# Joining the words of float64 weights on VectorE instead of GpSimd, in a transformer kernel on one core

## The chip, the core and the metric

The kernel runs on one core of a Trainium2 chip. A core has five engines, each with its own instruction queue, worked through in order: TensorE (PE in the profile, its weight loads PEld), VectorE (DVE), ScalarE (ACT), GpSimd (POOL) and SyncE (SP, which here issues transfers). Engines wait for each other by semaphores. The metric is the device time of one execution in microseconds (us).

## The reference

Eight batches of 576 tokens go through three layers, all in float32 (names as in the reference, shapes in brackets):

```
q_s = softmax(q) over d;  k_s = softmax(k) over the tokens      # 8 batches, 8 heads, 576 tokens, d = 64
x = (q_s @ (k_s^T @ v)), heads side by side                     # 576 x 512 for a batch
xn = (x - mean) / sqrt(var + 1e-6) * g_ln
x = x + relu(xn @ w_ch1) @ w_ch2                                # w_ch1 512 x 2048, w_ch2 2048 x 512
out = sum over 4 experts of gate * (causal attention of x) @ wo # the two best experts of each token count
```

`w_ch1` and `w_ch2` arrive as float64, which no engine computes in. The kernel reads them as pairs of 32-bit words and makes float32 numbers of them by integer operations.

## The kernel before, in words

Every float32 product is made of three fast products: an operand is split into a rounded upper part (ScalarE, a copy) and the rest, its lower part (a subtraction). The hidden layer's 2048 columns are 16 blocks `f` of 128. Phase 1 takes attention, normalisation and blocks 0 to 11 of the hidden layer for all batches; phase 2 takes the other blocks and the experts. For the last batch of phase 1 all 16 blocks are used.

**A block of weights** is 128 x 512 numbers (`Wide.pieces`); each `f` has two, one of `w_ch1` and one of `w_ch2`. Its steps: `size` (ScalarE, L245) takes the high word without its sign; `least` and `shift` (VectorE, L249, L253) bound it and rebase the exponent; `sign` (VectorE, L259) puts the sign back; `rest` (ScalarE, L256) rounds the low word to what is left of the mantissa; `whole` (L263, GpSimd) adds the two words as integers, here called **the join**; `big` (ScalarE, L266) makes the upper part; `small` (L270) makes the lower part, on VectorE for the blocks in `CDVE` and on GpSimd for the others. The first `Wide` has 24 blocks (numbers 0 to 23), converted at the start of the program; the second has 8 (numbered from 0 again), converted while the last batch of phase 1 is worked on.

**The start** (function `start`) covers the attention of batch 0 (pairs of heads 0 to 3), its normalisation, the 24 blocks, batch 0's products and, between them, the attention and normalisation of batch 1 (pairs 4 to 7). A planner in the program builds one list of operations with a cost for each, an engine and what each comes behind, and emits them by urgency; the order that it finds is then fixed for each engine (`in_order`), so an engine never passes a late instruction. The planner's costs are numbers in the code; changing one moves instructions.

The products of batch 0 come in 24 steps of about 3.2 us of TensorE: blocks 0 to 6 for the first half of the tokens (h = 0), the same for the second (h = 1), then blocks 7 to 11 for either half. In a step, `psh` is the first product, ScalarE and VectorE (L711, L714) make its two parts `hh`, and `acc` is the second product; L732 adds the sums to `x`. Step 18 (h = 0, block 11) is the last that needs newly converted weights.

**A normalisation** is the chain mean (`pmu`, TensorE) - subtract (L633, VectorE) - square (L639, ScalarE) - add up (L611, GpSimd) - split (`lnsum`, L615 and L618) - variance (`pvar`, TensorE) - root (L643 to L645, ScalarE) - refine (L650, L651, VectorE) - scale (L655, VectorE) - split into `xhl` (L660 ScalarE, L664 VectorE). The products of a half batch need its `xhl`.

**A pair of heads** needs the exponentials of q less their maximum, and their sums. For the pairs in `QACT` ScalarE does both in ten small instructions with an accumulator (L459); for the others GpSimd subtracts the maximum (L425), ScalarE takes one exponential (L437) and VectorE sums (L467).

Of the kernel before, what the change touches and what calls it, by code (L numbers as in the profile page):

```python
# [19 lines left out]
# Columns of the hidden layer (in blocks of 128) that the first phase works on; the second does the rest.  # L20
FSPLIT = 12
# Those of them that a batch's halves take in turn while the first batch is worked on
CHUNKS = (0, 7)
# Buffers of the blocks of weights that are being converted, and blocks loaded ahead of the one at work
TB, MIDB, AHEAD = 4, 4, 2
# Pairs of heads whose results come from float32 products, whose k loses its maximum on GpSimd, and whose exponentials
# of q come with their sums: at the start the other engines have more to do than the tensor engine.
WHOLE, KPOOL, QACT = 8, (0, 1, 5, 6, 7), (0, 1, 6, 7)
# Blocks of weights whose lower parts VectorE makes; GpSimd makes the rest.
CDVE = (1, 4, 7, 8, 9, 14, 16, 17, 18, 20, 21)  # L30
# Halves of batches (batch, half) whose means come from float32 products
DIRECT = ((0, 0),)
# The banks that come in turn for the first pairs of heads: the ring's, or one of the sums' before their first use
SPARE = (None, "acc0", "acc1", "acc2", None)
# The planner's times, in ns: of a step of the products, from one engine to another, behind loads; how much later than
# the first a more urgent piece may start, and one of these
# [4 lines left out]
# In which half-steps of the products the stages of a pair of heads and of a normalisation come, and from one of them  # L41
# to the next
UNIT_AT, UNIT_GAP = (0, 1, 2, 4, 5, 7), 4
NORM_AT, NORM_GAP = (0, 2, 4, 6, 8, 10), 8
# float32's least normal number: the first word of its float64 form, read as a float32
# [3 lines left out]
def weave(main, side):  # L49
    """Emits the pieces of `main`, with those of `side` spread evenly between them."""  # L50
    done = 0
    for i, piece in enumerate(main):
        piece()
        upto = (i + 1) * len(side) // len(main)
        for s in side[done:upto]:
            s()
        done = upto
    for s in side[done:]:
        s()


class Op:
    """A piece of work for one engine: about what it costs there and how long its result takes to the next engine, in ns,
    and what it comes behind."""
# [5 lines left out]
    def take(self, ring, *till):  # L70
        """Takes one of a ring's buffers, until `till` are done."""
        self.takes.append((ring, till))
        return self


def rush(ops):
    """Nothing but what these wait for is more urgent."""
    for op in ops:
        if op.end is None:
            op.late = min(op.late, RUSH)  # L80
            rush(op.deps)


def plan(ops, rings, which):
    """Has the pieces emitted in the order in which engines that do first what is most urgent would come to them."""
# [9 lines left out]
    while todo:  # L95
# [16 lines left out]
        # the most urgent piece of all that could start now, and then the most urgent one of its engine  # L112
# [17 lines left out]
def tile_kernel(ctx: ExitStack, tc: tile.TileContext, q, k, v, g_ln, w1, w2, w_gate, wq, wk, wv, wo, out):  # L130
# [15 lines left out]
    # Rows of a head in four interleaved chunks, and the last 128 of them in a fifth  # L146
# [17 lines left out]
    def in_order(instructions):  # L164
        """Each engine issues its instructions in this order."""
# [48 lines left out]
    class Wide:  # L214
        """Loads blocks of float64 numbers, as pairs of words with the low one first, rounds them to
        float32 and splits that."""
# [16 lines left out]
        def pieces(self):  # L233
            """The next block, piece by piece: the sign, the rebased exponent and the first 20 bits of the mantissa; the
            rest of it, rounded. Numbers under float32's normal range count as its least."""
# [26 lines left out]
            def whole():  # L262
                nc.gpsimd.tensor_tensor(box[0], box[0], low, op=ALU.add)  # L263
# [4 lines left out]
            def small():  # L268
                eng = nc.vector if n in CDVE else nc.gpsimd
                eng.tensor_tensor(lo, box[0].bitcast(F32), raw(h), op=ALU.subtract)  # L270
                while len(self.tiles) < min(n + 1 + self.ahead, len(self.blocks)):
                    self.load()
# [37 lines left out]
    # ------------------------------------------------------------------ phase 1  # L310
# [10 lines left out]
    def psy(name):  # L321
        if spare:
            # the sums' banks, before their first use
# [5 lines left out]
    # The first batch's last pairs of heads have buffers of their own, where weights lie later.  # L329
# [6 lines left out]
    def whole(n):  # L336
        """Whether a pair's result comes from float32 products: while the other engines have more to do than the tensor
        engine"""
# [18 lines left out]
    def next_unit(n):  # L357
        """The pair of heads that takes over a pair's buffers"""
# [36 lines left out]
    class Heads:  # L395
        """The linear attention of a pair of heads, in stages."""
# [16 lines left out]
        # Pieces of one engine's work each  # L413

        def k_rows(self):
            """The maximum of k's columns over each partition's rows"""
# [39 lines left out]
        def q_exps(self, j):  # L456
            """The exponentials, less the maximum, and their sums"""
# [23 lines left out]
        def q_parts(self, s):  # L481
            """The turned q, its rows back in order, as parts"""
# [34 lines left out]
        def kv_product(self):  # L517
            """k^T v, and the sums of k's columns"""
# [40 lines left out]
    def a_unit(n):  # L559
        """The work of a pair of heads, in stages, each behind the tensor engine's part of the last."""  # L560
# [31 lines left out]
    class Norm:  # L592
        """The normalisation of half a batch, in pieces of one engine's work each."""
# [8 lines left out]
        def add_x(self, c):  # L602
            """The sum of x's chunks"""
# [43 lines left out]
        def refine(self):  # L647
            """One Newton step to float32: r = r0 * (1.5 - 0.5 * ve * r0^2), here times -2"""
# [50 lines left out]
    class Step:  # L699
        """The products of half a batch with a block of the hidden layer, in pieces"""  # L700
# [27 lines left out]
        def add(self, c):  # L728
            """The residual and the sums so far"""
# [19 lines left out]
    def run_steps(steps, slots, wide):  # L749
        """The products of a list of (batch, half, block), the second of each behind the first of the next;  # L750
        slots: what else is emitted in each half of a step."""
# [23 lines left out]
    def front_slots(b):  # L775
        """When the stages of a batch's attention and normalisation are emitted, in halves of steps."""
# [49 lines left out]
    def start():  # L826
        """The first batch, the weights, and the second batch's attention and normalisation, as what is most urgent for
        the products comes first"""
# [16 lines left out]
        def unit(n):  # L845
# [22 lines left out]
            km = A("km", DVE, 740, head, [ldk, ldq])  # L868
# [45 lines left out]
            # no bank is held for want of a buffer  # L914
# [7 lines left out]
            # buffers  # L922
# [21 lines left out]
        def norm(b, h):  # L944
# [48 lines left out]
            # its reader comes later  # L993
            his[0].take("xhl", *([at["lastf", h]] if b == 0 else ()))

        # the weights
        nblocks = 2 * FSPLIT
        for k in range(nblocks):
# [11 lines left out]
            c0 = A(0, ACT, 520, g(0), [at.get(("w", k - 1, 0)), ld])  # L1010
            c1 = A(10, DVE, 340, g(1), [c0])
            c1 = A(1, DVE, 340, g(2), [c1])
            c2 = A(2, ACT, 520, g(3), [c0])
            c3 = A(3, DVE, 600, g(4), [c1])
            c5 = c4 = A(4, POOL, 1220, g(5), [c2, c3])
            c6 = A(6, ACT, 520, g(6), [c4])
            c7 = A(7, *((DVE, 600) if k in CDVE else (POOL, 1220)), g(7), [c6, at.get(("w", k - 1, 7))])
            c0.take("t", c7)
            ld.take("raw", c5)
        # the first batch's products  # L1020
# [33 lines left out]
        # the weights' second half lies where the first batch's buffers were  # L1054
# [7 lines left out]
        # From there on the sums' banks are theirs.  # L1062
# [73 lines left out]
    # ------------------------------------------------------------------ phase 2  # L1136
# [7 lines left out]
    # Adding 1e9 to the negated scores of later keys takes them out of the minimum.  # L1144
# [5 lines left out]
    # The last queries of two experts share the partitions; their mask, and their q between zeros.  # L1150
# [8 lines left out]
    # before[e, e'] = 1 where e' < e, after[e, e'] = 1 where e' > e  # L1159
# [21 lines left out]
    def mlp2(b, h, x2s):  # L1181
        """The rest of the feed-forward layers for half a batch, in pieces."""
# [36 lines left out]
    def psm(name):  # L1219
        """A bank; every so many come from those of the values' sums."""  # L1220
# [37 lines left out]
    def join(x2s, res):  # L1258
        """The block of tokens that lies in both halves"""
# [6 lines left out]
    def v_proj(x2s, res):  # L1266
        def one(c):
# [17 lines left out]
            # the last rows twice, for both parts of their weights  # L1285
# [8 lines left out]
        def gates(c0, c1):  # L1294
            """The top two of the experts' logits, and the softmax over them, for some blocks of tokens."""
# [34 lines left out]
    def layout(grp):  # L1330
        """Where the transposed weights of each block of keys lie, for the queries of a group."""
# [10 lines left out]
    class Unit:  # L1342
        """The attention of 128 queries over the earlier keys, for two experts."""
# [272 lines left out]
```

## Time and profile before

| | us |
|---|---|
| three runs: median | 1362.39 |
| lowest | 1358.6 |
| highest (disturbed) | 6870.57 |
| the profiled execution: its span (no other time of it is recorded) | 1355.0 |
| TensorE busy in the span | 1301.7 (96%) |
| VectorE, ScalarE, GpSimd busy | 888.9, 686.6, 343.5 |

The page's slices show where TensorE is not busy: the first four of 40 slices (about 135 us) have it at 5, 6, 7 and 8 tenths, and from there on it stands at 9 or more until the last slice. In the first four slices VectorE is at 7, 9, 9 and 9 tenths. So the time of the program is the time of the start, plus a stretch of some 1220 us in which TensorE is the limit and other engines do their work beside it. The lines shown further down are of three kinds: sums over a stretch, groups of equal instructions with their mean duration, and single instructions in order of time.

### The profile page before, as it was taken

How to read it: one execution, taken by the hardware profiler on the slowest of the kernel's cores; microseconds unless marked ns; L12 is line 12 of the kernel's file. 1: busy time of each engine (PE TensorE's matmuls, PEld its weight loads, DVE VectorE, ACT ScalarE, POOL GpSimd, SP SyncE). 2: the span in 40 equal slices, each digit the busy share in tenths (PEclk: the TensorE clock that was granted, in tenths of full speed). 3: DMA queues.
4: the chain of work that ended last, by engine and by line, in shares of the span. 5: the costliest groups of instructions: out<-in, count | busy, mean ns of one | idle time of the engine just before them, and what ended most of it. 6: DMA issues, size and time to landing. Idle time of an engine off the chain costs nothing.

```text
span 1355.0 us, 26225 instructions
## 1 busy us (share of the span) xinstructions
PE 1301.7 (96%) x9612; PEld 1268.8 (94%) x9612; DVE 888.9 (66%) x2602; ACT 686.6 (51%) x1802; POOL 343.5 (25%) x445
## 2 busy tenths in 40 slices
PE   5678999999999999999999999999999999999997
PEld 4577999999999999999999999999999999999996
DVE  7999564754645555545574238777768677776786
ACT  7667343443334433434442136656566656565666
POOL 5756323122121221212322002111211111121212
PEclk9889999999999999999999999999999999999999
DMA  8655232331321413315212023323232331423021
GB/s 230 198 173 150 80 111 56 117 94 45 110 75 67 109 58 123 84 50 158 65 34 48 1 77 126 107 82 106 82 97 87 86 105 59 115 86 90 23 67 55
DMA packets 136767, 124.78 MB, mean 92 GB/s; under 512 B 84160, under 2 KB 124096, under 8 KB 133056
## 3 DMA queue, kind: packets, MB, share of 16 engines
q1 hardware_dynamic: 126176, 97.16, 25.3%
q10 hardware_dynamic: 10464, 25.95, 5.2%
q8 instruction: 76, 1.25, 0.4%
q14 instruction: 51, 0.42, 0.1%
HBM read 74.07 MB, written 35.39 MB: 81 GB/s over the span
## 4 chain that ended last, share of the span: by engine, by line
PE 80%; DVE 12%; DMA 3%; ACT 2%; issue 1%; SPq 1%; POOL 1%; ACTq 0%; DVEq 0%; POOLq 0%
PE psh L174 25%; PE acc L174 19%; PE psqk L174 7%; PE psc L174 7%; PE pssc L174 4%; PE py L174 4%; PE psv L174 3%; PE pso L174 3%; PE pst L1401 2%; PE pkv L174 1%; DVE w_t L249 1%; DVE w_t L259 1%; PE po L174 1%; DMA q<-in_q_dram 1%; DVE km L418 1%
## 5 line engine op out<-in xcount | busy, mean ns | idle before, releaser
L174 PE MATMUL psh<-xhl,w 128*128 128x288 f32 x3072 | 468.3, 298 | 4.3 <-DVE w L270 2.2
L174 PEld LDWEIGHTS psh<-xhl,w 128*128 128x128 f32 x3072 | 428.3, 189 | 7.5 <-DVE w L270 2.5
L174 PE MATMUL acc<-hh,w 128*128 128x288 f32 x2400 | 370.4, 299 | 9.8 <-DVE hh L714 9.6
L174 PEld LDWEIGHTS acc<-hh,w 128*128 128x128 f32 x2400 | 335.6, 190 | 12.5 <-DVE hh L714 11.7
L714 DVE SCALAR_TENSOR_TENSOR hh<-psh,hh 128x288 fp32r<-128x288 f32 x200 | 90.4, 452 | 150.1 <-ACT hh L711 149.4
L711 ACT ACTIVATE hh<-psh 128x288 fp32r<-128x288 f32 x200 | 81.4, 408 | 181.8 <-PE psh L174 173.5
L1389 POOL TENSOR_SCALAR sm<-sm,st,lg 128x128 f32<-128x128 f32 (+3 forms) x128 | 80.3, 637 | 274.1 <-DVE st L1386 99.5
L174 PE MATMUL psqk<-x,wqk 128*128 128x288 f32 x768 | 112.6, 298 | 0.5 <-DVE lg L1289 0.3
L174 PEld LDWEIGHTS psqk<-x,wqk 128*128 128x128 f32 x768 | 104.7, 188 | 1.9 <-PE pst L1401 0.8
L174 PE MATMUL psc<-hb,w 128*128 128x288 f32 x672 | 100.5, 299 | 0.0
L1377 ACT ACTIVATE sm<-sm,st 128x128 f32<-128x128 f32 (+2 forms) x144 | 83.8, 583 | 18.5 <-DVE st L1369 17.4
L174 PEld LDWEIGHTS psc<-hb,w 128*128 128x128 f32 x672 | 92.4, 189 | 0.3
L1420 ACT ACTIVATE aTh<-pst 128x128 fp32r<-128x128 f32 (+5 forms) x254 | 79.2, 334 | 24.6 <-PE pst L1401 12.2
L1369 DVE CUSTOM_DVE_ANT_0 sm<-pssc,mask 128x128 f32<-128x128 f32 (+2 forms) x144 | 67.6, 482 | 32.8 <-PE pst L1401 20.1
L1421 DVE TENSOR_TENSOR aTl<-pst,aTh 128x384 fp32r<-128x384 f32 (+4 forms) x222 | 81.9, 382 | 10.0 <-ACT aTh L1420 7.5
L476 POOL TENSOR_TENSOR qe<-q,sm 128x320 f32<-128x320 f32 x64 | 47.8, 768 | 96.6 <-PE pkv L515 83.7
L611 POOL TENSOR_TENSOR sq<-sq 128x288 f32<-128x288 f32 x45 | 37.3, 828 | 111.2 <-ACT sq L639 109.3
L174 PE MATMUL py<-aTh,vv 128*128 128x320 f32 (+4 forms) x228 | 58.5, 275 | 1.6 <-DVE yf L1473 0.9
L174 PE MATMUL pssc<-k,q 128*128 128x128 f32 (+3 forms) x256 | 58.0, 327 | 0.5 <-DVE st L1369 0.5
L425 POOL TENSOR_TENSOR q<-q,sm 128x640 f32<-128x640 f32 x28 | 35.6, 1271 | 87.5 <-DVE sm L422 82.0
L263 POOL TENSOR_TENSOR w_t<-w_t,wraw 128x512 int32<-128x512 int32 x32 | 44.9, 1403 | 47.7 <-DVE w_t L259 10.7
L174 PE MATMUL psv<-wvg,x 128*128 128x260 f32 (+1 forms) x384 | 54.4, 285 | 0.0
(174 smaller groups left out, 2146.9 us busy)
## 6 DMA issues: line engine op xcount, KB each, us to landing
wraw<-in_moe_w_ch_dram SPq DMA_DIRECT2D x32, 512.0 KB, 3.9
xn_d<-xhl ACTq DMA_DIRECT2D x14, 1152.0 KB, 4.4
xhl<-xn_d SPq DMA_DIRECT2D x14, 1152.0 KB, 5.0
xp_d<-xT ACTq DMA_DIRECT2D x16, 576.0 KB, 3.6
k<-k SPq DMA_DIRECT2D x32, 288.0 KB, 3.9
k<-in_k_dram SPq DMA_DIRECT2D x32, 256.0 KB, 2.9
q<-in_q_dram SPq DMA_DIRECT2D x32, 256.0 KB, 3.4
out_dram<-ot SPq DMA_DIRECT2D x32, 256.0 KB, 2.0
```

What stands on the lines that cost most here:

```text
L174: nc.tensor.matmul(o, lhsT, rhs, start=start, stop=stop)
L263: nc.gpsimd.tensor_tensor(box[0], box[0], low, op=ALU.add)
L425: nc.gpsimd.tensor_tensor(self.q3, self.q3, self.sm[:, 0, :, None].to_broadcast([P, 2 * NCH, D]), op=ALU.subtract)
L476: nc.gpsimd.tensor_tensor(self.qe[:, :, j, :], self.qt[:, j], self.sm[:, 2, j * NCH:(j + 1) * NCH, None].to_broadcast([P, NCH, D]), op=ALU ...
L611: nc.gpsimd.tensor_tensor(self.t, self.t, self.sq[:, c], op=ALU.add)
L711: nc.scalar.activation(self.hh[:, 0], self.ps, AF.Relu)
L714: nc.vector.scalar_tensor_tensor(self.hh[:, 1], self.ps, 0.0, raw(self.hh[:, 0]), op0=ALU.max, op1=ALU.subtract)
L1369: nc.vector.tensor_tensor_reduce(out=sm[:m, c0:c1], in0=o_, in1=msk, scale=1.0, scalar=3e38 if n == 0 else st[:m, j, 0:1], op0=ALU.add, op ...
L1377: nc.scalar.activation(sm[:m, :w], sm[:m, :w], AF.Exp, bias=st[:m, j, last:last + 1], scale=-1.0, accum_out=st[:m, j, 2:3])
L1389: nc.gpsimd.tensor_scalar(sm[:m, :w], sm[:m, :w], st[:m, j, 3:4], self.gate()[:, j:j + 1], op0=ALU.mult, op1=ALU.mult)
L1420: nc.scalar.activation(oh, from_, AF.Copy)
L1421: nc.vector.tensor_tensor(ol, from_, raw(oh), op=ALU.subtract)
```

## The change

1. The join of all 32 blocks moves from GpSimd to VectorE. The program then holds, for an add of two int32 tensors on VectorE, an instruction of its own that works on 1,024 16-bit halves for each partition (it is printed as ISA, 128x1024, one instruction for a block).
2. The lower parts: before, VectorE made 11 of the first 24 and 3 of the last 8; now GpSimd makes those in `CPOOL`, which are 8 of the 24 and 2 of the 8, and VectorE makes 16 and 6.
3. `QACT` loses pairs 6 and 7: their q goes by GpSimd, one exponential, and VectorE's sum.
4. The planner's costs change (a k maximum, and all steps of a block), and with them the order of the start on every engine. Comments are dropped too.

```diff
-WHOLE, KPOOL, QACT = 8, (0, 1, 5, 6, 7), (0, 1, 6, 7)
+WHOLE, KPOOL, QACT = 8, (0, 1, 5, 6, 7), (0, 1)
-CDVE = (1, 4, 7, 8, 9, 14, 16, 17, 18, 20, 21)
+CPOOL = (2, 5, 8, 11, 14, 17, 20, 23, 24, 25, 26, 27, 28, 29, 30, 31)
...
             def whole():
-                nc.gpsimd.tensor_tensor(box[0], box[0], low, op=ALU.add)
+                nc.vector.tensor_tensor(box[0], box[0], low, op=ALU.add)
...
             def small():
-                eng = nc.vector if n in CDVE else nc.gpsimd
+                eng = nc.gpsimd if n in CPOOL else nc.vector
...
-            km = A("km", DVE, 740, head, [ldk, ldq])
+            km = A("km", DVE, 1230, head, [ldk, ldq])
...
-            c5 = c4 = A(4, POOL, 1220, g(5), [c2, c3])
-            c6 = A(6, ACT, 520, g(6), [c4])
-            c7 = A(7, *((DVE, 600) if k in CDVE else (POOL, 1220)), g(7), [c6, at.get(("w", k - 1, 7))])
+            c5 = c4 = A(4, DVE, 640, g(5), [c2, c3])
+            c6 = A(6, ACT, 580, g(6), [c4])
+            c7 = A(7, *((POOL, 1250) if k in CPOOL else (DVE, 640)), g(7), [c6, at.get(("w", k - 1, 7))])
```

Two places of the new order matter below. The first is VectorE ahead of batch 0's normalisation, which begins with L633. Before (`w_t_397`, `_421` and `_439` are the third, fourth and fifth block, their joins stand on GpSimd):

```order
L249 TENSOR_SCALAR w_t_397<-w_t_397 128x512
L253 TENSOR_SCALAR w_t_397<-w_t_397 128x512
L259 SCALAR_TENSOR_TENSOR w_t_397<-wraw_346,w_t_397 128x512
...
L253 TENSOR_SCALAR w_t_439<-w_t_439 128x512
L259 SCALAR_TENSOR_TENSOR w_t_439<-wraw_390,w_t_439 128x512
L270 TENSOR_TENSOR w2_0_155<-w_t_330,w2_0_155 128x512
L418 TENSOR_REDUCE km4_475<-k4_441 128x128
L633 TENSOR_TENSOR xc_487<-xT_334,pmu_399 128x288 x2
```

Now (`w_t_417` is the third block, `w_t_451` the fourth):

```order
L249 TENSOR_SCALAR w_t_417<-w_t_417 128x512
L253 TENSOR_SCALAR w_t_417<-w_t_417 128x512
L259 SCALAR_TENSOR_TENSOR w_t_417<-wraw_338,w_t_417 128x512
L270 TENSOR_TENSOR w1_0_154<-w_t_272,w1_0_154 128x512
L263 ISA w_t_417<-wraw_338,w_t_417 128x1024
L249 TENSOR_SCALAR w_t_451<-w_t_451 128x512
L253 TENSOR_SCALAR w_t_451<-w_t_451 128x512
L633 TENSOR_TENSOR xc_469<-xT_335,pmu_427 128x288
```

Ahead of L633 stood five `sign` steps, one lower part and a fifth k maximum; now there are three `sign` steps, three joins and one lower part, and the k maximum comes later.

The second place is TensorE at the end of batch 0, where the variance `pvar` of batch 1's first half stands (`xhl_930` and `xhl_878` are batch 0's second half, `xhl_1738` and `xhl_1772` batch 1's first half). Before:

```order
L174 MATMUL psh_1669<-xhl_930,w1_9_513 128x288 x12
L174 MATMUL pvar_1683<-lnsum_1667,mean_r_83 128x288 x2
L174 MATMUL acc0_1647<-hh_1645,w2_8_512 128x288 x3
...
L174 MATMUL psh_1742<-xhl_930,w1_11_517 128x288 x12
L174 MATMUL acc0_1647<-hh_1735,w2_10_516 128x288 x3
...
L174 MATMUL psh_1825<-xhl_1738,w1_0_154 128x288 x12
L174 MATMUL acc0_1647<-hh_1772,w2_11_518 128x288 x3
```

Now:

```order
L174 MATMUL psh_1710<-xhl_878,w1_11_508 128x288 x12
...
L174 MATMUL acc0_1630<-hh_1735,w2_11_509 128x288 x3
...
L174 MATMUL acc3_1633<-hh_1735,w2_11_509 128x288 x3
L174 MATMUL pmu_1750<-lnsum_1663,mean_r_83 128x288 x2
L174 MATMUL pvar_1761<-lnsum_1754,mean_r_83 128x288 x2
L174 MATMUL psh_1809<-xhl_1772,w1_0_154 128x288
L174 MATMUL psh_1835<-xhl_1772,w1_1_156 128x288
```

Before, `pvar` stood with three steps of products behind it, ahead of the first one that reads its result; now it stands behind the last product of batch 0, with nothing between it and the product that reads its result. VectorE agrees with that. The last sums of batch 0 and the variance's input, now:

```order
L732 TENSOR_TENSOR xT_335<-xT_335,acc2_1632 128x288
L618 TENSOR_TENSOR lnsum_1754<-sq_1621,lnsum_1754 128x288
L732 TENSOR_TENSOR xT_335<-xT_335,acc3_1633 128x288
L650 SCALAR_TENSOR_TENSOR sq_1621<-pvar_1761,sq_1621 128x288
L651 SCALAR_TENSOR_TENSOR sq_1621<-sq_1621 128x288
L655 SCALAR_TENSOR_TENSOR xc_1618<-xc_1618,g_sb_87,sq_1621 128x288 x4
L664 TENSOR_TENSOR xhl_1772<-xc_1618,xhl_1772 128x576 x2
```

The input `lnsum_1754` of the variance has moved behind the addition of `acc2`, that is, behind a product of batch 0's last step; before, it stood ahead of all four of those additions.

## Rows read from the trace of the kernel before

**Rows 1.** The page's first line: span and instructions.
```profile
span 1355.0 us, 26225 instructions
```
**Rows 2.** Stretches of the span: length, then each engine's busy time, clock, DMA share.
```profile
core 0: us, PE busy (x) PEld busy (x) DVE busy (x) ACT busy (x) POOL busy (x), PEclk, DMA share, GB/s
0.00:37.00 37.00, 20.20 (x93) 14.83 (x93) 28.84 (x55) 29.00 (x86) 21.84 (x34) 0.95 0.87 234
37.00:50.70 13.70, 6.49 (x21) 4.28 (x22) 13.60 (x24) 9.33 (x22) 10.23 (x8) 0.74 0.66 195
50.70:138.30 87.60, 71.57 (x489) 68.17 (x489) 83.83 (x135) 59.72 (x148) 58.15 (x47) 0.94 0.52 164
138.30:165.00 26.70, 26.70 (x199) 26.37 (x198) 14.91 (x32) 10.37 (x23) 8.19 (x10) 1.00 0.19 70
...
600.00:760.00 160.00, 157.37 (x1190) 155.93 (x1189) 86.87 (x175) 62.89 (x134) 39.94 (x43) 1.00 0.23 68
```
**Rows 3.** VectorE to 140 us, by form: busy us, mean ns, idle before.
```profile
L259 DVE SCALAR_TENSOR_TENSOR w_t<-wraw,w_t 128x512 int32<-128x512 int32 x24 | 20.3, 846 | 0.4
L249 DVE TENSOR_SCALAR w_t<-w_t 128x512 f32<-128x512 f32 x24 | 19.3, 806 | 1.8 <-ACT w_t L245 1.8
L253 DVE TENSOR_SCALAR w_t<-w_t 128x512 int32<-128x512 int32 x24 | 17.4, 727 | 0.3
L270 DVE TENSOR_TENSOR w<-w_t,w 128x512 fp32r<-128x512 f32 x11 | 13.2, 1203 | 0.2 <-ACT w L266 0.2
L418 DVE TENSOR_REDUCE km<-k 128x128 f32<-128x640 f32 x9 | 11.5, 1273 | 3.3 <-DMA k<-in_k_dram 3.3
...
L655 DVE SCALAR_TENSOR_TENSOR xc<-xc,g_sb,sq 128x288 f32<-128x288 f32 x8 | 6.9, 908 | 0.0
L467 DVE TENSOR_REDUCE sm<-q 128x10 f32<-128x640 f32 x5 | 4.0, 805 | 0.0
```
**Rows 4.** VectorE in order of time: start us, duration us, what.
```profile
29.13 0.69 DVE L259 SCALAR_TENSOR_TENSOR w_t<-wraw,w_t 128x512 int32<-128x512 int32 x1
29.74 0.42 DVE L249 TENSOR_SCALAR w_t<-w_t 128x512 f32<-128x512 f32 x1
...
30.35 0.41 DVE L253 TENSOR_SCALAR w_t<-w_t 128x512 int32<-128x512 int32 x1
30.79 1.65 DVE L259 SCALAR_TENSOR_TENSOR w_t<-wraw,w_t 128x512 int32<-128x512 int32 x1
```
**Rows 5.** GpSimd in order of time, the same stretch.
```profile
30.58 1.31 POOL L263 TENSOR_TENSOR w_t<-w_t,wraw 128x512 int32<-128x512 int32 x1 [2.23 <-ACT wraw L256]
```
**Rows 6.** GpSimd to 140 us, by form.
```profile
L263 POOL TENSOR_TENSOR w_t<-w_t,wraw 128x512 int32<-128x512 int32 x24 | 33.1, 1380 | 29.9 <-ACT wraw L256 8.4 <-DVE w_t L259 7.7 <-ACT hh L711 5.0
L270 POOL TENSOR_TENSOR w<-w_t,w 128x512 fp32r<-128x512 f32 x13 | 19.8, 1526 | 1.6 <-ACT w L266 1.6
...
L425 POOL TENSOR_TENSOR q<-q,sm 128x640 f32<-128x640 f32 x6 | 7.9, 1312 | 0.2 <-DVE sm L422 0.2
```
**Rows 7.** GpSimd's last lower part of the start, in order of time.
```profile
139.40 1.29 POOL L270 TENSOR_TENSOR w<-w_t,w 128x512 fp32r<-128x512 f32 x1
```
**Rows 8.** All engines in order of time: batch 1's first normalisation from its variance.
```profile
151.23 0.43 PE L174 MATMUL pvar<-lnsum,mean_r 128*128 128x288 f32 x2
...
154.21 1.80 DVE L655 SCALAR_TENSOR_TENSOR xc<-xc,g_sb,sq 128x288 f32<-128x288 f32 x4
...
155.19 0.69 ACT L660 ACTIVATE xhl<-xc 128x576 fp32r<-128x576 f32 x1
...
156.30 0.74 DVE L664 TENSOR_TENSOR xhl<-xc,xhl 128x576 fp32r<-128x576 f32 x1
```
**Rows 9.** TensorE in order of time, behind an idle time and later.
```profile
84.82 3.01 PE L174 MATMUL acc<-hh,w 128*128 128x288 f32 x11 [4.39 <-DVE hh L714]
...
91.03 1.84 PE L174 MATMUL acc<-hh,w 128*128 128x288 f32 x12
```
**Rows 10.** VectorE's custom instruction of phase 2, whole span, two of its forms.
```profile
L1369 DVE CUSTOM_DVE_ANT_0 sm<-pssc,mask 128x512 f32<-128x512 f32 x32 | 21.2, 685 | 9.5 <-PE pst L1401 8.2 <-PE pst L1450 0.6 <-POOL sm L1389 0.5
...
L1369 DVE CUSTOM_DVE_ANT_0 sm<-pssc,mask 128x128 f32<-128x128 f32 x32 | 8.7, 283 | 3.9 <-PE pssc L174 3.6
```

More of the change, by code (lines that the diff above doesn't have):

```diff
@@ L1009, in start @@
             ld = add(("w", k, "ld"), SP, 1450, wide.load, [at.get(("w", k - 1, "ld"))], lat=1100)
[L1010 to L1014, printed above, removed]
-            c5 = c4 = A(4, POOL, 1220, g(5), [c2, c3])
-            c6 = A(6, ACT, 520, g(6), [c4])
-            c7 = A(7, *((DVE, 600) if k in CDVE else (POOL, 1220)), g(7), [c6, at.get(("w", k - 1, 7))])
+            c0 = A(0, ACT, 620, g(0), [at.get(("w", k - 1, 0)), ld])
+            c1 = A(10, DVE, 360, g(1), [c0])
+            c1 = A(1, DVE, 360, g(2), [c1])
+            c2 = A(2, ACT, 620, g(3), [c0])
+            c3 = A(3, DVE, 640, g(4), [c1])
+            c5 = c4 = A(4, DVE, 640, g(5), [c2, c3])
+            c6 = A(6, ACT, 580, g(6), [c4])
+            c7 = A(7, *((POOL, 1250) if k in CPOOL else (DVE, 640)), g(7), [c6, at.get(("w", k - 1, 7))])
             c0.take("t", c7)
```

## The prediction

> **What bounds the kernel now.** I read the page's slices first: TensorE has idle time in the first four of forty, and hardly any after. Then the sums over stretches [rows 2] say who has none there. From 37 to 50.7 us VectorE is busy 13.60 of 13.70 us, from 50.7 to 138.3 us 83.83 of 87.60, while TensorE has 71.57, ScalarE 59.72 and GpSimd 58.15. From 138.3 to 165 us TensorE is busy all 26.70 us. 138.3 is where step 18 begins, the last that needs a new block. So VectorE's work, up to the last block, sets when TensorE can start its stretch without gaps; behind that, TensorE sets everything. What a change does here is therefore two numbers: how much later or earlier VectorE is done with the blocks, and how much idle time comes into the stretch behind them.
>
> Much of VectorE's busy time is not work. Its `sign` step takes 0.69 us undisturbed and 1.65 us one block later [rows 4], and in those 1.65 us a join runs on GpSimd, 30.58 to 31.89 [rows 5]. The means to 140 us [rows 3] against the clean durations (`least` 0.42, `shift` 0.41 [rows 4]; L655 0.45, a quarter of 1.80 [rows 8]) give what VectorE is held: `sign` 24 x (846 - 690) = 3.7 us, `least` 24 x (806 - 420) = 9.3, `shift` 24 x (727 - 410) = 7.6, lower parts 11 x (1203 - 690) = 5.6, L655 8 x (908 - 450) = 3.7; together 30.0 us. GpSimd is busy 21.84 + 10.23 + 58.15 = 90.2 us [rows 2] in that time. I take the ratio as a price: VectorE is held 0.33 us for each us that GpSimd works.
>
> The Trainium skill (SBUF — State Buffer, "SBUF: two separate sides") says that the two share a port pair as an exclusive lock, whose loser is blocked fully, and counts VectorE instructions with two SBUF inputs among those that want it. The 1.65 us agree. By that rule joins on VectorE are held as `sign` is, 24 x 0.156 = 3.7 us more than below, and the time would be about 1373.
>
> **The price of a join on VectorE.** The trace of before has none. Low end: 0.69 us, the clean `sign` step [rows 4], which also takes 512 words from two tensors, one of them the same strided words. High end: VectorE's custom instruction takes 685 ns for 512 elements and 283 for 128 [rows 10], so 1.047 ns an element and 149 ns fixed; 1,024 halves one by one are 1.22 us. I take 0.69, because `sign` is the nearest row: same tensors, same words. An instruction's end overlaps the next one's start: 29.13 + 0.69 is 0.08 past 29.74 [rows 4]. So VectorE pays 0.61 for `sign`, join or lower part, 0.34 and 0.33 for `least` and `shift`.
>
> **To batch 0's `xhl` (50.7 us).** By the first shown order, VectorE has up to there two `least`, one `shift`, one `sign` and one k maximum less, one lower part, four joins and one more of q's small steps (which I cost at nothing) more. With 1.19 us for a k maximum undisturbed (estimate from 1273 less a little holding [rows 3]): -0.68 - 0.33 - 0.61 - 1.19 + 0.61 + 2.44 = +0.2; the missing q's maximum (0.73, by the like reduction of 805 [rows 3] less holding) makes it -0.5. GpSimd loses six joins and two lower parts there, 6 x 1.38 + 2 x 1.53 = 11.3 us [rows 6], times 0.33 is 3.7 us less holding. `xhl` comes 4.2 us earlier, at 46.5.
>
> **From there to the last block.** Before, the last `sign` step began at 133.0, about 83 us behind 50.7 with its own 0.61. Now VectorE has 20 joins more (12.2 us), four lower parts (2.4; of 24 it makes 16, not 11, and one of the five came earlier), the `least`, `shift` and `sign` left over (1.6), the k and q maxima left over (1.9) and q's sums of two pairs (2 x 0.73 = 1.5): +19.6. GpSimd loses 18 joins (24.8) and three lower parts (4.6) and gains two L425 of 1.31 (2.6): -26.8 us, times 0.33 is 8.8 less holding. So 83 + 19.6 - 8.8 = 93.8 us, and the last join ends at 46.5 + 93.8 = 140.3. Behind it come the upper part (0.69 by a 576-element copy [rows 8]), GpSimd's lower part (1.29 [rows 7]) and the handovers: about 2.2 us, 142.5. Before, the last lower part of the start ended at 139.40 + 1.29 = 140.7 [rows 7]. **Term 1: +1.8 us.** ScalarE's twenty small exponentials of two pairs go away and two large ones come; I cost that at nothing, since VectorE's work covers it (59.72 of 87.60 busy), and if that cover goes it is a gain.
>
> **Behind the last block.** The second and third shown orders bring something new. Before, `pvar` of batch 1's first half had three steps of products behind it. Now nothing stands between it and the first product that reads its `xhl`. TensorE passes nothing, so it waits out the chain: `pvar` ended at 151.66, and L655 runs to 156.01, the first of two L664 takes 0.74 behind it [rows 8], some 5.1 us from `pvar`'s end to the lower `xhl`. TensorE has 0.3 us of work of that from the upper part (done at 155.88). Ahead of `pvar` it also waits for `lnsum`, which VectorE has behind the addition of `acc2`: about 0.5 us. So 5.3 us idle. An idle time of that size has slower products behind it: after 4.39 idle 11 matmuls took 3.01 us, later 12 took 1.84, that is 1.69 for 11 [rows 9]: +1.3. **Term 2: +6.6 us.**
>
> **The last 8 blocks** are converted beside batch 7's products: eight joins (4.9 us) and three lower parts (1.8) more on VectorE, in 160 us of which VectorE is busy 86.87 and TensorE 157.37 [rows 2]. I cost this at nothing; its cover is VectorE's idle 73 us. If VectorE there is late for `hh`, TensorE waits for it; between -2.6 (all TensorE idle time of that stretch) and, with the same 2.6 again, +2.6.
>
> **Sum.** The profiled execution's span is 1355.0 [rows 1]; 1355.0 + 1.8 + 6.6 = 1363.4. The runs shown stand above that span, the lowest by 3.6 and the median by 7.4; I add the mean, 5.5: **1369 us**, against a median of 1362.4.
>
> **Rivals.** *One block's chain is what waits, not the sum of VectorE's work* (faster). Then every join costs what its step costs in the chain, 1.38 on GpSimd [rows 6] against 0.69: 24 x 0.69 = 16.6 us saved, the wait at `pvar` stays, 1355 - 16.6 + 6.6 + 5.5 = 1350.5. The same comes if holding falls by 0.55 and not 0.33 us for each of the 38.1 us that GpSimd loses (11.3 + 26.8). For it: VectorE's `least`, `shift` and lower parts are held by far more than a join alone overlaps. Against: VectorE idles only 3.8 of 87.60 us, so hardly anything waits for a chain. Its point of decision is whether VectorE has idle time ahead of 138 us. Chance 0.22.
>
> The Trainium skill (GPSIMD Engine Reference, "4.1 Engine selection") has two-input elementwise work about twice as slow on GpSimd and gives it to VectorE. 1.38 against 0.69 would agree, but no row of before has the join on VectorE, and the page does not ask which engine is full.
>
> *A join takes 1.22 us* (slower): halves go one by one, 24 x 0.53 = 12.7 us more in the stretch that VectorE bounds: 1381.6. For it: 1,024 elements are printed for it, and custom instructions do one element in 1.047 ns. Against: nothing but that. It decides wherever VectorE has no idle time, and above 0.69 each 0.1 us costs 2.4. Chance 0.15.
>
> *The wait at `pvar` does not come*, because the last products of batch 0 are themselves held up or `lnsum` is early: the order leaves no room for it, 1362.4 by the sum without term 2. Chance 0.03.
>
> Forecast: 0.60.
>
> **Range and chances.** 2% of the median is 27 us, about what a measurement of this kernel can tell from no change. The range goes from the first rival to the second: 1349 to 1382; outside lie both beyond their own values, less than 2 in 10. Faster by over 2% would be below 1335: with 6.6 lost at `pvar`, 34 us of the about 39 that TensorE idles to 138.3 us (16.80 + 7.21 + 16.03 [rows 2] = 40.0) would have to go, 0.03. Slower by over 2%, above 1389.6: the second rival with holding that does not fall at all (12.5 us more, 1394), 0.04. Within 2%: 0.93.
>
> **What to look for.** In the changed kernel's profile: the join's mean on VectorE, 0.69 or above, less the holding; the means of `least` and `shift`, which should fall by about 0.33 us for each us that GpSimd lost; VectorE still busy nearly all of the time to the last block; the last lower part of the start at about 142.5; TensorE idle for about 5 us between `pvar` and the first `psh` of batch 1, with slower products behind; and the stretch of the last 8 blocks as before. The forecast is wrong if VectorE has idle time ahead of the last block (then the first rival), if the join is over 0.9 us, or if TensorE has no idle time at batch 1's first product.

## The result, and the profile after

The changed kernel takes **1371.2 us** (median; 1368.9 to 1372.5) against 1361.1 before: a ratio of 1.0074, 95% interval 1.0058 to 1.009. It is slower by 0.7%; the forecast was 1369. The page's first line, against [rows 1]:

```profile
span 1369.2 us, 26152 instructions
```

The run that was profiled took 1370.99 us, so 1.8 us lie around its span. Sums over stretches of the changed kernel, against [rows 2]:

```profile
core 0: us, PE busy (x) PEld busy (x) DVE busy (x) ACT busy (x) POOL busy (x), PEclk, DMA share, GB/s
37.00:50.70 13.70, 7.72 (x33) 6.09 (x31) 13.46 (x24) 8.88 (x19) 4.86 (x4) 0.75 0.65 185
50.70:138.30 87.60, 71.82 (x468) 66.91 (x467) 85.14 (x152) 55.53 (x109) 38.82 (x30) 0.92 0.55 168
...
600.00:760.00 160.00, 158.77 (x1204) 157.81 (x1204) 91.09 (x191) 66.98 (x140) 25.25 (x27) 1.00 0.25 75
```

VectorE still has hardly any idle time ahead of the last block (85.14 of 87.60 us busy; 83.83 before). GpSimd fell from 58.15 to 38.82 us there. VectorE by form, to 145 us, against [rows 3]:

```profile
L259 DVE SCALAR_TENSOR_TENSOR w_t<-wraw,w_t 128x512 int32<-128x512 int32 x24 | 20.3, 845 | 0.2
L263 DVE CUSTOM_DVE_ANT_0 w_t<-wraw,w_t 128x1024 uint16<-128x1024 uint16 x24 | 19.6, 818 | 0.6 <-ACT wraw L256 0.4
L249 DVE TENSOR_SCALAR w_t<-w_t 128x512 f32<-128x512 f32 x24 | 15.1, 630 | 3.4 <-ACT w_t L245 3.4
L253 DVE TENSOR_SCALAR w_t<-w_t 128x512 int32<-128x512 int32 x24 | 13.6, 565 | 0.3
L270 DVE TENSOR_TENSOR w<-w_t,w 128x512 fp32r<-128x512 f32 x16 | 12.6, 787 | 0.0
...
L655 DVE SCALAR_TENSOR_TENSOR xc<-xc,g_sb,sq 128x288 f32<-128x288 f32 x8 | 3.9, 514 | 0.0
```

`least` fell from 806 to 630 ns, `shift` from 727 to 565, the lower parts from 1203 to 787; `sign` stayed at 845. Two joins while GpSimd stood idle show the clean price, in order of time (start, duration):

```profile
25.31 0.67 DVE L263 CUSTOM_DVE_ANT_0 w_t<-wraw,w_t 128x1024 uint16<-128x1024 uint16 x1
26.72 0.69 DVE L263 CUSTOM_DVE_ANT_0 w_t<-wraw,w_t 128x1024 uint16<-128x1024 uint16 x1
```

Worked out as in the prediction, VectorE is held 3.7 + 5.0 + 3.7 + 1.6 + 0.5 us in these forms and 24 x (818 - 690) = 3.1 in the joins, 17.6 us in all, where it was 30.0.

The end of the start and what stands behind it, TensorE and the chain it waits for, in order of time (start, duration, engine, line; in brackets the idle time ahead and who ended it):

```profile
142.30 1.28 DVE L263 CUSTOM_DVE_ANT_0 w_t<-wraw,w_t 128x1024 uint16<-128x1024 uint16 x1
144.32 1.28 POOL L270 TENSOR_TENSOR w<-w_t,w 128x512 fp32r<-128x512 f32 x1 [1.29 <-ACT w L266]
...
153.80 1.79 POOL L611 TENSOR_TENSOR sq<-sq 128x288 f32<-128x288 f32 x2
153.87 0.45 ACT L615 ACTIVATE lnsum<-x_sum 128x288 fp32r<-128x288 f32 x1 [0.41 <-POOL x_sum L606]
...
160.22 1.75 PE L174 MATMUL psh<-xhl,w 128*128 128x288 f32 x12
161.80 3.33 PE L174 MATMUL acc<-hh,w 128*128 128x288 f32 x24
164.97 0.43 PE L174 MATMUL pmu<-lnsum,mean_r 128*128 128x288 f32 x2
165.48 0.44 ACT L615 ACTIVATE lnsum<-sq 128x288 fp32r<-128x288 f32 x1 [3.07 <-PE pmu L174]
165.98 0.89 PE L174 MATMUL pvar<-lnsum,mean_r 128*128 128x288 f32 x2 [0.58 <-ACT lnsum L615]
...
170.83 0.68 ACT L660 ACTIVATE xhl<-xc 128x576 fp32r<-128x576 f32 x1 [2.00 <-DVE xc L655]
171.57 5.45 PE L174 MATMUL psh<-xhl,w 128*128 128x288 f32 x24 [4.70 <-ACT xhl L660]
```

The last join ends at 143.6 and the last lower part at 145.6 (140.7 before, [rows 7]). TensorE stands idle 0.58 us ahead of `pvar` and 4.70 behind it. And the rows say why: GpSimd has the sum of squares of batch 1's first half at 155.59, but the copy of it into `lnsum` (L615) starts at 165.48, just behind the end of `pmu`. `lnsum` has one buffer (the planner's `rings` have `"lnsum": 1`, as before the change). Since 153.87 it held the sum of the *second* half, whose `pmu` stands on TensorE behind the last product of batch 0. The second L615 waits for that, and `pvar` for the second L615 and its lower part. A stretch just behind the wait:

```profile
171.50:175.20 3.70, 3.63 (x14) 3.32 (x15) 3.00 (x5) 1.91 (x4) 0.39 (x1) 0.50 0.38 157
```

The granted clock is 0.50, which is the level of 1.2 GHz, after 4.70 us without work: 14 products take the 3.70 us, where 24 took 3.33 at 161.80.

### The profile page after: what moved, and what is told of

Same layout as the page of the kernel before. It is cut to its first block, busy times and chain, and to the rows that moved or that the text cites. A ratio compares the mean times of both kernels' runs of the same rounds, so it can differ in the third digit from the quotient of the medians.

```text
span 1369.2 us, 26152 instructions
## 1 busy us (share of the span) xinstructions
PE 1313.0 (96%) x9612; PEld 1276.8 (93%) x9612; DVE 894.0 (65%) x2642; ACT 682.4 (50%) x1764; POOL 296.3 (22%) x407
## 4 chain that ended last, share of the span: by engine, by line
PE 70%; DVE 3%; DMA 2%; ACT 1%; issue 0%; POOL 0%; SPq 0%; ACTq 0%; DVEq 0%; POOLq 0%
PE psh L174 21%; PE acc L174 15%; PE psqk L174 7%; PE psc L174 7%; PE pssc L174 4%; PE py L174 4%; PE psv L174 4%; PE pso L174 3%; PE pst L1401 2%; PE pkv L174 1%; PE po L174 1%; DMA k<-in_k_dram 1%; DMA q<-in_q_dram 1%; PE pst L1450 1%; DVE km L418 0%
## 5 line engine op out<-in xcount | busy, mean ns | idle before, releaser
L174 PE MATMUL psh<-xhl,w 128*128 128x288 f32 x3072 | 475.9, 300 | 13.0 <-DVE w L270 7.2
L174 PEld LDWEIGHTS psh<-xhl,w 128*128 128x128 f32 x3072 | 433.6, 191 | 17.3 <-DVE w L270 8.4
L1377 ACT ACTIVATE sm<-sm,st 128x128 f32<-128x128 f32 (+2 forms) x144 | 83.7, 583 | 18.5 <-DVE st L1369 17.3
L1421 DVE TENSOR_TENSOR aTl<-pst,aTh 128x384 fp32r<-128x384 f32 (+4 forms) x222 | 82.0, 382 | 10.1 <-ACT aTh L1420 7.5
L476 POOL TENSOR_TENSOR qe<-q,sm 128x320 f32<-128x320 f32 x64 | 50.5, 808 | 110.8 <-PE pkv L515 86.8
L425 POOL TENSOR_TENSOR q<-q,sm 128x640 f32<-128x640 f32 x30 | 38.8, 1293 | 102.0 <-DVE sm L422 90.8
L1401 PE MATMUL pst<-ident,sm 128*128 128x128 f32 x320 | 52.9, 276 | 0.0
```

Source lines behind the costliest of these rows:

```text
L174: nc.tensor.matmul(o, lhsT, rhs, start=start, stop=stop)
L425: nc.gpsimd.tensor_tensor(self.q3, self.q3, self.sm[:, 0, :, None].to_broadcast([P, 2 * NCH, D]), op=ALU.subtract)
L476: nc.gpsimd.tensor_tensor(self.qe[:, :, j, :], self.qt[:, j], self.sm[:, 2, j * NCH:(j + 1) * NCH, None].to_broadcast([P, NCH, D]), op=ALU ...
L1377: nc.scalar.activation(sm[:m, :w], sm[:m, :w], AF.Exp, bias=st[:m, j, last:last + 1], scale=-1.0, accum_out=st[:m, j, 2:3])
L1401: nc.tensor.transpose(pt[:kw, kb * m:kb * m + m], sm[:m, kb * P:kb * P + kw], ident[:m, :m])
L1421: nc.vector.tensor_tensor(ol, from_, raw(oh), op=ALU.subtract)
```

## Experiments

The table has the kernels in the order of the argument; each ratio is to the kernel before, run on the same chip (its medians 1361.1 to 1362.0).

| kernel | us | ratio (95%) |
|---|---|---|
| join alone, old order | 1355.0 | 0.9955 (0.9943 to 0.9967) |
| and the planner told | 1358.6 | 0.9983 (0.9971 to 0.9995) |
| and all its new costs | 1357.8 | 0.9975 (0.9963 to 0.9987) |
| and the lower parts | 1359.3 | 0.9979 (0.9965 to 0.9993) |
| the whole change, variance first | 1361.9 | 1.000 (0.9989 to 1.001) |
| the whole change | 1371.2 | 1.0074 (1.0058 to 1.009) |

**1. The join alone.**
```diff
-                nc.gpsimd.tensor_tensor(box[0], box[0], low, op=ALU.add)
+                nc.vector.tensor_tensor(box[0], box[0], low, op=ALU.add)
```


> The kernel before with one line changed: the join goes to VectorE; the lower parts, q's exponentials and the planner's costs stay as before, so each engine's order is the old one, and pvar keeps its three steps of products behind it. Theory (VectorE's work to the last block sets the start, GpSimd's work holds it at 0.33 us per us): VectorE +24 x 0.61 = 14.6 us, GpSimd -33.1 us x 0.33 = -10.9, so +3.7 us and no wait at pvar: about 1365 us against 1361. Rival (the chain of one block sets the start): 24 x 0.69 = 16.6 us faster, about 1344.

Measured 1355.0: between the two (1365 and 1344), and a gain. Its first trace was of an execution of 1359.15 us, so a second was taken:

> The join alone in the old order once more, for a second trace: the first one was of an execution 4 us above the median of that kernel. If those 4 us are slower products in the middle of the program, the start is as in the first trace (step 18 at 137.4 us) and the stretch behind it shorter.

That run took 1355.23 us with a span of 1353.3. Step 18 began at 136.2, not 137.4: the 4 us were in part in the start. VectorE by form to 145 us, and GpSimd's last lower part of the start in order of time:

```profile
L263 DVE CUSTOM_DVE_ANT_0 w_t<-wraw,w_t 128x1024 uint16<-128x1024 uint16 x24 | 19.8, 825 | 0.4 <-ACT wraw L256 0.3
L259 DVE SCALAR_TENSOR_TENSOR w_t<-wraw,w_t 128x512 int32<-128x512 int32 x24 | 17.8, 742 | 0.4
L253 DVE TENSOR_SCALAR w_t<-w_t 128x512 int32<-128x512 int32 x24 | 15.4, 641 | 0.2
L249 DVE TENSOR_SCALAR w_t<-w_t 128x512 f32<-128x512 f32 x24 | 12.6, 524 | 1.1 <-ACT w_t L245 1.1
L270 DVE TENSOR_TENSOR w<-w_t,w 128x512 fp32r<-128x512 f32 x11 | 8.0, 731 | 0.2 <-ACT w L266 0.2
L655 DVE SCALAR_TENSOR_TENSOR xc<-xc,g_sb,sq 128x288 f32<-128x288 f32 x8 | 5.1, 672 | 0.0
```
```profile
134.69 1.28 POOL L270 TENSOR_TENSOR w<-w_t,w 128x512 fp32r<-128x512 f32 x1
```

Held: 3.2 + 1.2 + 5.5 + 2.5 + 0.5 + 1.8 = 14.7 us, 15.3 less than before, for 31 us less of GpSimd to 145 us (64.0 against 94.9): 0.49 us for each, not 0.33. So VectorE's account is +14.6 - 15.3, about even. The tail got shorter too: before, the last lower part ended 7.0 us behind the last `sign` step (133.7 to 140.7), because GpSimd's queue had a join, another block's lower part, two L476 and an L425 ahead of it; here the last join ends at 133.0 and the last lower part at 136.0. But TensorE is not shown to have waited for that lower part before: in neither trace of before does it idle between 130 us and step 18, and it begins step 18 at 139.0 us in one and at 140.4 in the other, though the lower part is there at 140.7 and 140.6. What is shown is less idle time of TensorE up to step 18: 35.5 us (37.3 in the first trace of the join alone), where it was 138.97 - 98.93 = 40.0 before and 40.2 in the second trace of before. Stretches to step 18's first product, of the kernel before (twice) and of the join alone, columns as above:

```profile
0.00:138.97 138.97, 98.93 (x606) 87.90 (x607) 126.27 (x211) 98.05 (x255) 90.89 (x89) 0.93 0.63 185
0.00:140.44 140.44, 100.26 (x606) 89.25 (x607) 125.71 (x212) 98.73 (x256) 92.41 (x90) 0.91 0.63 183
0.00:136.23 136.23, 100.73 (x606) 88.60 (x607) 124.13 (x234) 97.89 (x255) 59.72 (x66) 0.94 0.67 189
```

Of TensorE's waits from 50 to 140 us, the one for `kvw`, which the attention of batch 1 makes, fell most:

```profile
PE po L174 <- ACT kvw L537: 4.7, 2, 2.7
PE po L174 <- ACT kvw L537: 1.8, 2, 1.6
```

(Total, times, longest; first before, then the join alone.) Which of VectorE's instructions brought that was not tried. Another 1 us lies with the last 8 blocks: from 600 to 760 us TensorE idles 1.7 us, where it idled 2.6 and 2.7.

**2. All but the join** (the changed kernel, that line back on GpSimd, and its cost in the planner).

> The changed kernel with the join back on GpSimd (and the planner told so); the lower parts by CPOOL and two pairs in QACT stay. In its order pvar again has products behind it. Theory: VectorE +5 lower parts (3.0 us) and +2 sums of q (1.5), GpSimd -5 x 1.53 + 2 x 1.31 = -5.0 us, x 0.33 = -1.7: +2.8 us, about 1364 us. Rival (the loss of the change is in the lower parts and q, not in the join and its order): 1371 us, as the changed kernel.

1366.1, a ratio of 1.0039 (1.0026 to 1.0051): a loss of 4.7, more than the 2.8 of the sum and less than the rival's 1371, without any wait at batch 1's `pvar`. In its trace TensorE waits 2.66 us for `kvw` and begins step 18 at 147.2 us, later than in any trace above; why is not shown.

**3. Parts added one by one to the join.** The planner told of it, in the kernel before with the join on VectorE:
```diff
-            c5 = c4 = A(4, POOL, 1220, g(5), [c2, c3])
+            c5 = c4 = A(4, DVE, 640, g(5), [c2, c3])
```


> The kernel before with the join on VectorE and the planner told so (DVE, 640), its other costs, the lower parts and q as before. Against the join alone in the old order (1355 us) only the order differs. If the order is of no account: 1355. If planning with the join on VectorE is what loses, because the last join now stands behind other work of VectorE (the last sums of x of batch 1) and step 18 waits for it: about 1359, as with the changed kernel's costs and four pairs.

1358.6: the new order loses 3.6. At 147.3 us TensorE waits 1.60 us for a `hh` that VectorE makes behind the last `sign` and join, and these stand behind the subtraction (L633) of batch 1's normalisation (the last join ends at 148.5, with the join alone at 133.0). That is 1.60 of the 3.6 us, and the trace of the next kernel has the same 1.60. Then the changed kernel with the lower parts and q of before, and with q alone of before (`QACT = (0, 1, 6, 7)`):

> The changed kernel with the lower parts and q as before (11 of 24 lower parts on VectorE, four pairs in QACT): join and all planner's costs remain of the change. Against the one with 16 lower parts on VectorE (1359 us): VectorE -5 x 0.61 = -3.0 us, GpSimd +5 x 1.5 = 7.5 us, times 0.33 to 0.5 = +2.5 to +3.7: 1359 us within 1. If more lower parts on VectorE were a loss of their own: 1355.

> The changed kernel with QACT as before, four pairs on ScalarE. The order it gives has pvar with products behind it again. Theory (VectorE sets the start, and the wait at pvar is the other loss): VectorE -1.5 us, GpSimd -2.6 x 0.33 = -0.9, no wait at pvar -7: about 1362 us. Rival (ScalarE's forty small exponentials would hold up the blocks' upper parts, so the change to two pairs was a gain): 1371 us or above.

1357.8 and 1359.3: 1.2 and 2.7 us below what was expected; neither rival (1355; 1371 or above) came. Only the last part, two pairs instead of four, loses much: 12 us.

**4. Is it q's work, or the order?** The changed kernel's order, with q of pairs 6 and 7 on ScalarE at the same places:
```diff
+                sc = n in (6, 7)
-                qb = A("qb", POOL, 1220, f("q_below"), [qm])
+                qb = A("qb", POOL, 1220, f("q_neg") if sc else f("q_below"), [qm])
...
```


> The changed kernel with the work of q for pairs 6 and 7 back on ScalarE, but at the same places of the order: GpSimd's subtraction becomes VectorE's small negation, the one exponential the ten small ones, VectorE's sum nothing. pvar stays behind the last product of batch 0. If the 12 us between the changed kernel (1371) and the one with four pairs (1359) come from the order, that is from the wait at pvar: about 1369 us (VectorE -1.5, holding -0.9). If they come from the work of the two pairs: about 1359 us.

1373.6, a ratio of 1.0095 (1.0066 to 1.0123): no faster than the changed kernel, though 1369 was expected. So the 12 us come from the order, not from the work of the two pairs. TensorE in its trace:

```profile
167.15 0.90 PE L174 MATMUL pvar<-lnsum,mean_r 128*128 128x288 f32 x2 [0.86 <-ACT lnsum L615]
172.73 3.58 PE L174 MATMUL psh<-xhl,w 128*128 128x288 f32 x12 [4.69 <-ACT xhl L660]
```

**5. The wait at `pvar` taken away.** First by a due time:
```diff
-            at["hl", 1, h].late = total + h * FSPLIT * STEP - STEP
+            at["hl", 1, h].late = total + h * FSPLIT * STEP - (3 if h == 0 else 1) * STEP
```


> The changed kernel with one number of the planner's due times changed: batch 1's first normalisation is due two steps earlier. In the order it gives, pvar has five of batch 0's products and more behind it, and the last join stands behind that normalisation on VectorE. Theory (the idle time at pvar, 5.3 us, and the slow products behind it, about 2 us, are a loss of their own): about 1364 us. Rival (the idle time only moves: the last block comes later by the normalisation's work on VectorE, and TensorE waits for that): 1371 us or more.

1366.5: between the two, nearer to the theory's time. The rival was right that the wait moves: VectorE makes the last block behind batch 1's normalisation, and TensorE waits for that block:

```profile
158.05 1.06 DVE L263 CUSTOM_DVE_ANT_0 w_t<-wraw,w_t 128x1024 uint16<-128x1024 uint16 x1
159.15 0.63 ACT L266 ACTIVATE w<-w_t 128x512 fp32r<-128x512 f32 x1 [2.38 <-DVE w_t L263]
159.83 0.85 PE L174 MATMUL acc<-hh,w 128*128 128x288 f32 x2 [5.37 <-ACT w L266]
```

Then by what the rows of the changed kernel point to, who holds the buffer of `lnsum`:
```diff
+        at["ln", 1, 1, ("pmu", "high")].deps.append(at["ln", 1, 0, ("pvar", "mean")])
```


> The changed kernel with one dependency more in the planner: the parts of the sum of batch 1's second half (its pmu) come behind the first half's pvar. In the changed kernel's trace the one buffer of lnsum holds the second half's sum from 154 us until that pmu is done at 165.4, behind the last product of batch 0, though GpSimd has the first half's sum of squares ready at 155.6. The order up to the last join is that of the changed kernel; pvar now has two steps of products behind it. If the buffer's holder makes the wait: 5.3 us idle and about 2 us of slower products go, 1364 us. If the wait only comes back elsewhere, as with the normalisation due earlier: 1367 to 1371.

1361.9: 9.3 us less than the changed kernel, and no difference from the kernel before (1361.98 beside it). A second buffer for `lnsum` was not tried. The copy now starts as soon as the sum is there, and `pvar` runs between products:

```profile
153.88 1.69 POOL L611 TENSOR_TENSOR sq<-sq 128x288 f32<-128x288 f32 x2
155.61 0.45 ACT L615 ACTIVATE lnsum<-sq 128x288 fp32r<-128x288 f32 x1 [2.06 <-POOL sq L611]
158.72 0.43 PE L174 MATMUL pvar<-lnsum,mean_r 128*128 128x288 f32 x2
```

**6. What paces the start.** Two kernels, each the join alone with one edit more: `sign` done twice (first edit, its loop's body left out here), and all lower parts of the start on VectorE (second edit):
```diff
+                for _ in range(2 if len(self.blocks) > 8 else 1):
...
-                eng = nc.vector if n in CDVE else nc.gpsimd
+                eng = nc.vector if n in CDVE or len(self.blocks) > 8 else nc.gpsimd
```


> The join alone in the old order, and the sign step of the first 24 blocks done twice (the second changes nothing): VectorE +24 x 0.61 = 14.6 us. If VectorE's work paces the start: +14.6 less what idle time it has from 50 to 133 us (3.7), so +11 to +15: 1366 to 1370. If something else paces it (ScalarE's steps, the handovers, TensorE): under +4, below 1359.

1375.5, so +20.5 against the join alone, more than the work added, and all of it in the start: TensorE begins step 18 at 156.5 us, 20.3 later. So VectorE's work paces the start. The 48 `sign` steps (L260 there), to 152 us:

```profile
L260 DVE SCALAR_TENSOR_TENSOR w_t<-wraw,w_t 128x512 int32<-128x512 int32 x48 | 37.8, 787 | 1.2
```

They take 787 ns each against 742. Holding in the same six forms is about 18.5 us against 14.7, with GpSimd's work as before, so it does not go by GpSimd's time alone; the last 2 us were not followed.

> The join alone in the old order, and all 24 lower parts of the start on VectorE at the same places: VectorE +13 x 0.61 = 7.9 us, GpSimd -13 x 1.5 = -19.5 us. With holding of 0.33 us for each us of GpSimd (the forecast's price): -6.4, so +1.5 us: 1356.5. With 0.53 (the price that the join alone showed, 30.0 to 14.2 us of holding for about 30 us of GpSimd): -10.3, 1352.6. With 0.24 (what is left in that kernel over GpSimd's work): -4.7, 1358.

1356.6, a ratio of 0.9963 (0.9945 to 0.998): +1.6 us, as the forecast's price would have it. But its trace does not have that price: 19 us less of GpSimd (44.9 against 64.0) give 3.7 us less holding (11.0 against 14.7), 0.19 for each, and 7.9 - 3.7 is 4.2 us, not 1.6. The match with 0.33 is luck, and what makes up the other 2.6 us is not shown.

**7. The kernel before again.**

> The kernel before once more, for a second trace of it: how far its start and the waits behind it differ from one execution to the next. If they do not, the last product of batch 0's step 18 begins at 139 us and the span is 1355; if the start varies, the difference between the traces of before and of the join alone has to be read with that.

1359.37 us, span 1357.6, step 18 at 140.4: five idle times of TensorE between 60 and 130 us (1.8, 2.2, 4.4, 2.7 and 2.0) are the same to 0.05 us as in the first trace, and behind the last two the clock is another (the last section). A sixth, ahead of a `pvar` at 76 us, is 2.75 us where it was 1.24. So the start does vary, by 1.5 us at step 18, and a difference of that size between two traces shows nothing.

## Why the prediction was right

The time was right; of the terms some were, and two errors balanced. Against the median of before, the two terms said +8.4 us, and +10.1 came.

**VectorE bounds the start.** Right: 85.14 of 87.60 us busy, and work added to it makes the program longer by no less than that work (14.6 us of doubled `sign` steps: +20.5, experiment 6).

**The join's price.** Right: where GpSimd is idle a join takes 0.67 to 0.69 us; the forecast had taken 0.69 from `sign`. The rival of 1.22 us is out. By the rule on the shared port pair (the Trainium skill, SBUF — State Buffer, "SBUF: two separate sides") a join, with its two inputs, is held as `sign` is, which the forecast put at 24 x 0.156 = 3.7 us; the trace has 24 x 0.128 = 3.1 us and agrees.

**Term 1, +1.8 us.** Right in sign, too small in its own measure. `xhl` came at 48.0, not 46.5; the last join at 143.6, not 140.3; the lower part 2.0 us behind it, as said. So the last lower part came 4.9 us later than before (145.6 against 140.7), not 1.8. TensorE lost less by it: step 18's first product begins at 142.1 against 139.0 and 140.4 in the two traces of before, +3.1 and +1.7. The fall in holding, 12.5 us by the forecast, was 12.4. The way to the loss was not quite the forecast's, either:

```profile
0.00:142.09 142.09, 105.86 (x607) 93.06 (x607) 128.49 (x238) 94.30 (x217) 60.04 (x64) 0.91 0.63 181
```

TensorE's idle time up to step 18 is 36.2 us, less than the 40.0 and 40.2 of before; it comes there later because it is busy 5.6 to 6.9 us longer on as many products. Which of them take longer, and why, was not followed.

The price of 0.33 us of holding for each us of GpSimd was a mean over unlike work. Joins alone gave 0.49, lower parts taken away after them 0.19; whether the kind of instruction makes the difference, or that less holding was left by then, is not shown. That step failed where the join stands by itself: 1365 was expected, 1355.0 came. Of these 10 us, 4.4 are holding (15.3 us less, not 10.9) and 1 the last 8 blocks. For the rest the tail is a candidate, which the forecast priced in the changed kernel (2.2 us) and not as the 7 us that the old one had, but no run shows TensorE waiting for it.

**Term 2, +6.6 us.** The mechanism was right, its size too small. From step 23's first product to batch 2's, the changed kernel (first line) and the one with the variance first:

```profile
160.22:263.91 103.69, 95.63 (x707) 93.63 (x705) 55.52 (x120) 38.47 (x83) 20.34 (x25) 0.97 0.27 80
160.60:256.10 95.50, 93.43 (x705) 91.87 (x704) 55.78 (x120) 37.09 (x81) 20.42 (x25) 1.00 0.27 84
```

103.7 against 95.5 us: 8.2, of which 6.0 are idle time and 2.2 are products that take longer. The idle time at `pvar` was as said (0.58 + 4.70 = 5.3), though it ended with the upper part of `xhl` and not, as the forecast had it, with the lower; half the clock on 14 products cost 1.85, not 1.3; the rest is in other waits. What failed in this step is the reason given for the wait ahead of `pvar`: not VectorE's addition of `acc2`, but the one buffer of `lnsum`, which also sets where the planner can place `pvar`.

**The last 8 blocks, 0.** A small gain: TensorE idles 1.23 of 160 us, where the two traces of before have 2.63 and 2.73. The range of ±2.6 held it.

**What lies around the span, 5.5 us.** Wrong by 3.7: it is 1.7 to 2.1 in the runs that were profiled here. The forecast set one execution's span against the median of others, and 1355.0 + 1.8 = 1356.8 is below all of them. The span was forecast 5.8 us short (1363.4 for 1369.2), and the two errors nearly cancelled: that the forecast lands within 2.2 us of the measured time is in part luck.

**The rivals.** One block's chain did not decide for the whole change: VectorE has hardly any idle time, which was its point of decision. For the join alone it had the direction, not the size (6.4 us of the 16.6) and not the mechanism: there, too, VectorE is busy nearly all the time to the end of the last join, 79.99 of the 82.30 us from 50.7 to 133.0. The forecast's second way to this rival does not add up. To reach 1350.5 from 1368.9, holding would have to fall by 0.81 us and not by 0.55 for each of the 38.1 us of GpSimd, which is 31 us in all, more than the 30.0 there were; 0.55 is worth 8.4 us.

The Trainium skill (GPSIMD Engine Reference, "4.1 Engine selection") gives such an add to VectorE as about twice as fast; 1.38 against 0.68 us agrees, and here the full engine was the right place.

What stays open: where TensorE's longer busy time ahead of step 18 comes from; where the 3.6 us go that the planner's new order loses with the join alone (1.60 was read from traces, nothing was tried); and why all but the join costs 4.7 us.

## What to carry to other kernels

An engine that is full can still take work from another, if that work was holding it: count what the move frees beside what it adds, and price it by a run that moves this instruction alone; a mean over all of the other engine's work (0.33 here) was off for either kind (0.49 and 0.19). Where a planner fixes the order, change one part at a time with the order kept: here one line in the old order gains 0.45%, and the same line with its re-planned surroundings loses 0.7%. When a chain starts late, look at who still holds the buffer that it writes, before moving its due time.

## What was not expected of the hardware

The clock behind an idle time is not the same from one execution to the next. In the same place, after the same idle time, the changed kernel and the one with the variance first show (TensorE in order of time):

```profile
138.74 3.01 PE L174 MATMUL acc<-hh,w 128*128 128x288 f32 x11 [2.95 <-DVE hh L714]
```
```profile
139.35 1.73 PE L174 MATMUL acc<-hh,w 128*128 128x288 f32 x11 [2.94 <-DVE hh L714]
```

2.95 and 2.94 us idle, then 11 products in 3.01 at a granted clock of 0.50, or in 1.73 at 1.00. The kernel before does it too, in its two traces:

```profile
116.38 0.75 PE L174 MATMUL po<-qT,kvw 128*128 128x288 f32 x2 [2.68 <-ACT kvw L537]
116.29 1.33 PE L174 MATMUL po<-qT,kvw 128*128 128x288 f32 x2 [2.70 <-ACT kvw L537]
```

2.68 and 2.70 us idle, then the clock 1.00 in one execution and 0.50 in the other. In the place above it is worth 1.3 us, so some of the 2 to 4 us between runs of one kernel can be this. It also means that the forecast's price for slower products behind an idle time (1.3 us, from one place in one execution) could not be sure.

And holding goes both ways. A lower part on GpSimd in the changed kernel, while VectorE did one two-tensor instruction right behind another:

```profile
66.00 3.61 POOL L270 TENSOR_TENSOR w<-w_t,w 128x512 fp32r<-128x512 f32 x1 [4.93 <-ACT w L266]
```
```profile
66.59 0.68 DVE L270 TENSOR_TENSOR w<-w_t,w 128x512 fp32r<-128x512 f32 x1
67.19 0.68 DVE L263 CUSTOM_DVE_ANT_0 w_t<-wraw,w_t 128x1024 uint16<-128x1024 uint16 x1
67.80 0.68 DVE L259 SCALAR_TENSOR_TENSOR w_t<-wraw,w_t 128x512 int32<-128x512 int32 x1
```

GpSimd took 3.61 us for what took 1.28 at 144.32, and VectorE's three took their clean 0.68.
